# A fused scan and channel-mixer kernel: block 1 of x loaded ahead of w1, b1 from another queue, C loaded behind the first DMA transposes

## Chip, cores, metric

The kernel runs on one core of one Trainium2 chip. The metric is device time in microseconds of one execution. The kernel before was run three times: 159.55, 159.99 and 160.57 us, median 159.99. A further execution was profiled; the times in the views come from that one.

## What is computed

The input x has 2048 rows of 448. It is normalised along the row to xn. One branch (A) is a complex diagonal recurrence over the rows, the other (B) a channel mixer with a second normalisation; their product is added to x:

```python
def _A_ref(x, Lambda_re, Lambda_im, B_re, B_im, C_re, C_im, log_dt, Dskip):
    ...
    Lam_bar = jnp.exp(dt * Lam)
    B_bar = ((Lam_bar - 1.0) / Lam)[:, None] * Bmat
    Bu = jnp.einsum("bld,pd->blp", x + 0j, B_bar)
    ...
    for t in range(L):
        h = Lam_bar[None, :] * h + Bu[:, t, :]
        hs.append(h)
    ...
    y = 2.0 * jnp.einsum("blp,dp->bld", hseq, Cmat).real + x * Dskip[None, None, :]
    return y

def _B_ref(x, w1, b1, w2, b2):
    y = _layernorm(x, axis=-1)
    h = _gelu(jnp.einsum("bsd,df->bsf", y, w1) + b1)
    return jnp.einsum("bsf,fd->bsd", h, w2) + b2

x = A_x
xn = _layernorm(x, axis=-1)
s = _A_ref(xn, ...)
g = _silu(_B_ref(xn, B_w1, B_b1, B_w2, B_b2))
return x + s * g
```

Inputs and output are bfloat16.

## The kernel before

**Tiling.** The rows are cut into 8 blocks of 256 rows; a block lies on 128 partitions as 128 even and 128 odd rows (`par` 0 and 1). Two blocks form a group, and there are 4 groups. The program's loop over groups emits, for each, the statistics and the two normalised forms of x (`xn` for branch A, `xn2`, called `xm` in the keys, for branch B), their transposes (`xnT`, `xn2T`), the products with B (`bu`, L616), the recurrence as scans (`ssm`, L641), the first mixer product with GELU (`mm1`, L686 and L692), the second mixer product (`mm2`, L715), and the output of the recurrence with the final sum (`ym`, L747 to L759).

**Group 0 is different.** Its first mixer product is cut in halves by block (`mm1_half`, L701 and L707): all seven pairs of columns for block 0, then all seven for block 1, so that it can begin when block 0 alone is there. Block 0 is normalised by `first_norm`, each half as soon as it has landed, and transposed on TensorE (L380). Block 1 is normalised by `ln_stats`, `ln_scale` and `ln_apply` on VectorE and transposed by eight matmuls on TensorE (`xt`, L440), whose result VectorE copies out of bank 6 (L446).

**Weights and loads.** w1 is loaded in four chunks of its columns (`ldw1`), each as two DMAs, one of 384 rows (keys `w1_0` to `w1_3`) and one of the remaining 64 (`w1r_0` to `w1r_3`). The bias b1 is one more row of the same tile, on partition 64 (key `w1b`), and every first-mixer product reads it, so every L701 task needs it. The tile's lower half is zeroed first (L293). B comes in four DMAs (`Bn`), w2 in four, C in three (`ldc`, into a part of `gT` that is free at that time; keys `Cn0`, `Cn512`, `Cn448`). Nearly all loads go out from SyncE, in one hardware queue. The four parameter vectors (`vrows`) go out from ScalarE's queue, ahead of its first table load.

**DMA transposes.** VectorE and ScalarE make the scaled B matrices (`lb`, L566 to L569); each is then transposed by a DMA on SyncE (`bt`, keys `BT0` to `BT6`, L83). The transposes of xn for group 0 (`xnT0_0`, `xnT0_1`) and all later transposes of xn and xm are DMA transposes on SyncE as well, and so are those of C (`ct_dma`, keys `Ct0` to `Ct3`). L83 and L84 are the two issuing lines of the helper `dma`; all DMAs carry one of them.

**Order.** All work is a list of tasks, numbered in the order in which the program makes them. A hand-written list, `ORDER`, gives the order in which they are emitted; each engine runs its own tasks in that order. `SECOND` names the tasks that take their second engine. `link` finds what each task depends on from the keys that it reads and writes, and `emit` puts a wait on a semaphore ahead of a task where its engine has not yet seen that the other is done. A wait stops everything behind it on that engine; for SyncE this is every later DMA.

SyncE's order in the start-up, by keys: `x0p0`, `x0p1` (the two halves of block 0), `w1_0`, `w1r_0`, `w1b` (b1), `x1`, `w1_1`, `w1r_1`, `w1_2`, `w1r_2`, `w1_3`, `w1r_3`, four of `Bn`, four of w2, `x2` with `x3` (one DMA), `Cn0`, `Cn512`, `BT3`, `Cn448`, `xnT0_1`, `BT0`, `xnT0_0`, then the two transposes of xm for group 1, then `Ct3`, `Ct0`, `Ct2`, `Ct1`.

TensorE's order: warm-up, parameters, block 0's transposes, six halves of `mm1_half` for block 0, block 1's transposes (task 113), the seventh half for block 0, seven for block 1, four `mm2` of group 0, `bu` with `BT3` and `BT0`, `mm1` of group 1. The chunks are used by two halves each (the last by one).

The lines for the scaled identity `De` (L530 on ScalarE, L531 on VectorE), used by `m0` (L605, L607) with CQ, are part of the start-up too: `De0` and `De1` on VectorE, `De3` and `De2` on ScalarE between GELUs.

Of the kernel before, what the change touches and what calls it, by code (L numbers as in the profile page):

```python
# [17 lines left out]
class Task:  # L18

    __slots__ = ("eng", "ins", "reads", "writes", "sem", "idx", "deps", "chain", "alts")

    def __init__(self, eng, ins, reads, writes, sem):
        self.eng, self.ins, self.reads, self.writes, self.sem = eng, ins, tuple(reads), tuple(writes), sem
        self.deps = set()
        self.chain = False
        self.alts = [(eng, ins)]

    def choose(self, k):  # L30
# [5 lines left out]
class Plan:  # L36
# [4 lines left out]
    def __init__(self, nc):  # L41
        self.nc = nc
        self.engs = {"pe": nc.tensor, "act": nc.scalar, "dve": nc.vector, "pool": nc.gpsimd, "sp": nc.sync}
        self.tasks = []
        self.sems, self.counts, self.cms = {}, {}, []
        for e in ("pe", "act", "dve", "pool"):
            self._sem(e)
        self.seen = {e: {} for e in ENGS}
        self.ndma = 0

    def _sem(self, name):
# [9 lines left out]
    def add(self, eng, ins, reads=(), writes=(), dur=0.2, lat=0.1, prio=0.0, sem=None, chain=False, table=None, mode=None):  # L61
        if callable(ins):
            ins = [ins]
        t = Task(eng, ins, reads, writes, sem or eng)
        t.idx = len(self.tasks)
        t.chain = chain
        self.tasks.append(t)
        return t

# [35 lines left out]

    def emit(self):
        self.link()
        for k in SECOND:
            self.tasks[k].choose(1)
        order = [self.tasks[k] for k in ORDER]  # L110
        assert len(order) == len(set(order)) == len(self.tasks)
        done = {}
        for t in order:
            eng, seen = self.engs[t.eng], self.seen[t.eng]
            need = {}
            for d in t.deps:
                sem, val = done[d]
                if need.get(sem, 0) < val:
                    need[sem] = val
            for sem, val in need.items():  # L120
                if seen.get(sem, 0) < val:
                    eng.wait_ge(self.sems[sem], val)
                    seen[sem] = val
            for k, fn in enumerate(t.ins):
                last = fn(eng)
                if t.chain and k < len(t.ins) - 1:
                    self.counts[t.eng] += 1
                    last.then_inc(self.sems[t.eng], 1)
                    eng.wait_ge(self.sems[t.eng], self.counts[t.eng])
                    seen[t.eng] = self.counts[t.eng]  # L130
            inc = 16 if t.sem not in ENGS else 1
            self.counts[t.sem] += inc
            last.then_inc(self.sems[t.sem], inc)
            done[t] = (t.sem, self.counts[t.sem])
        for sem, val in self.counts.items():
            if val and self.seen["sp"].get(sem, 0) < val:
                self.nc.sync.wait_ge(self.sems[sem], val)


def dram_ap(t, offset, ap):  # L140
    return bass.AP(tensor=t.tensor, offset=offset, ap=ap)
# [1 line left out]

ORDER = [int(k) for k in """
# [17 lines left out]
""".split()]  # L164
SECOND = [int(k) for k in """
44 143 144 148 150 168 172 174 178 180 198 200 204 220 230 232 289 290 317 328 402 404 429 434 435 438 511 512 513 538 539 541 542 544 545 607 611 630
# [12 lines left out]
def bass_recurrent_scan__ssm_conv_s5__mixer_channel_mlp__prompt_kernel(  # L179
# [12 lines left out]
    L, D, F = 2048, 448, 1792  # L192
# [5 lines left out]
    with ExitStack() as es:  # L198
        def SB(name, shape, dtype=BF):
            return es.enter_context(nc.sbuf_tensor(name, shape, dtype))  # L200
# [12 lines left out]
        w1_sb = SB("w1_sb", [128, 4, F])  # L213
# [60 lines left out]
        with nc.Block():  # L274
# [28 lines left out]
            def ld(eng, o, i, writes, nbytes, prio, reads=(), dur=0.45):  # L303
                kb.dma(eng, o, i, reads=reads, writes=writes, prio=prio, nbytes=nbytes, dur=dur)
# [4 lines left out]
            def ldx(b0, n, prio, reads=(), eng="sp"):  # L309
                ld(eng, x_all[:, b0:b0 + n, :, :], dram_ap(A_x, b0 * 256 * D, [[2 * D, 128], [256 * D, n], [D, 2], [1, D]]),  # L310
                   [f"x{b}" for b in range(b0, b0 + n)], n * 256 * D * 2, prio, reads, dur=0.25 + 0.2 * n)
# [10 lines left out]
            S1 = 10 * PINNED  # L322
# [1 line left out]
                ld("sp", x_all[:, 0, par, :], dram_ap(A_x, par * D, [[2 * D, 128], [1, D]]), [f"x0p{par}"], 114688, S1)  # L324
            ldw1(0, S1 + 1)
            ldx(1, 1, S1 + 2)
            ld("sp", w1_sb[64:65, 3, :], dram_ap(B_b1, 0, [[F, 1], [1, F]]), ["w1b"], 4000, S1 + 1)
            for c in (1, 2, 3):
                ldw1(c, S1 + 3)
            for ri, bm in enumerate((A_B_re, A_B_im)):  # L330
# [539 lines left out]
```

## Time and profile before

| | |
|---|---|
| runs: median (lowest to highest) | 159.99 us (159.55 to 160.57) |
| profiled execution, first to last instruction | 159.2 us |
| mean granted TensorE clock | 0.996 |
| TensorE busy | 151.3 us (95%) |
| VectorE busy | 136.9 us (86%) |
| ScalarE busy | 93.2 us (59%) |
| GpSimd busy | 51.5 us (32%) |
| DMA | 14.70 MB, mean 92 GB/s over the span |

Engines in the views: PE is TensorE, DVE VectorE, ACT ScalarE, POOL GpSimd, SP SyncE; a q behind the name is the engine's sequencer, which issues DMAs. In a timeline a row has the start, the length, the engine, the line, the operation, the tiles, the count, and in square brackets the idle time of the engine just before and what ended it. In a list of waits a row has the total, the number of times and the longest. A DMA row ends with the time from issue to landing. The names of tiles are those of the memory: the tiles w1 and w2 both appear as `w_sb`, and the loads of C as `gT`.

### The profile page before, as it was taken

What the parts mean: (1) busy time and instruction counts of PE and PEld (TensorE: products, weight loads), DVE (VectorE), ACT (ScalarE), POOL (GpSimd) and SP (SyncE); (2) the same over time, 40 slices, a digit from 0 to 9 for tenths busy, and PEclk for the clock granted to TensorE, in tenths of its full rate; (3) what the DMA queues carried; (4) which work ended last, traced back from release to release, by engine and by line L of the source; (5) the groups of instructions that cost most, each with busy time, mean ns of one, the idle gap of its engine ahead of it and who ended that gap; (6) DMA issues with size and microseconds to landing.
All of it is one profiled execution on the core that took longest, in us unless ns stands there. A gap on an engine that the chain in (4) does not pass through costs nothing.

```text
span 159.2 us, 2725 instructions
## 1 busy us (share of the span) xinstructions
PE 151.3 (95%) x946; PEld 93.7 (59%) x946; DVE 136.9 (86%) x265; ACT 93.2 (59%) x151; POOL 51.5 (32%) x127
## 2 busy tenths in 40 slices
PE   6959999999999999999999999999989999999990
PEld 6849965565565556566655555576556655555560
DVE  5478969999998799999789999893999599999982
ACT  3839899997779962689835472212456972450200
POOL 5578840007616000038600573302015420060021
PEclk9999999999999999999999999999999999999998
DMA  4999999888980057000210430213401000010032
GB/s 103 260 303 364 315 149 198 139 161 159 276 172 4 0 100 147 0 0 4 48 20 0 120 65 1 57 21 94 116 4 58 0 4 0 0 58 0 0 115 60
DMA packets 31174, 14.70 MB, mean 92 GB/s; under 512 B 24693, under 2 KB 30713, under 8 KB 31162
## 3 DMA queue, kind: packets, MB, share of 16 engines
q1 hardware_dynamic: 30914, 14.26, 39.4%
q0 software_dynamic: 96, 0.23, 0.4%
q8 instruction: 7, 0.11, 0.3%
q10 hardware_dynamic: 152, 0.05, 0.1%
q14 instruction: 5, 0.04, 0.1%
HBM read 6.89 MB, written 1.84 MB: 55 GB/s over the span
## 4 chain that ended last, share of the span: by engine, by line
PE 88%; DMA 7%; SPq 2%; DVE 1%; issue 0%
PE psum L715 27%; PE psum L686 21%; PE psum L616 13%; PE psum L747 12%; PE psum L701 7%; PE psum L750 4%; DMA w_sb<-in_B_w_dram 4%; PE psum L605 3%; DMA xnT<-xn_sb 3%; SPq L84 2%; PE psum L753 1%; PE psum L440 0%; DVE t L756 0%; DVE tmp L759 0%; PE psum L607 0%
## 5 line engine op out<-in xcount | busy, mean ns | idle before, releaser
L715 PE MATMUL psum<-w_sb,gT 128*128 128x448 bf16 x224 | 43.8, 352 | 0.0
L686 PE MATMUL psum<-xn2T,w_sb 128*128 128x512 bf16 x168 | 38.2, 379 | 0.1
L715 PEld LDWEIGHTS psum<-w_sb,gT 128*128 128x128 bf16 x224 | 21.9, 98 | 20.0
L692 ACT ACTIVATE gT<-psum 128x1024 bf16<-128x1024 f32 x21 | 21.4, 1021 | 11.7 <-PE psum L686 11.6
L686 PEld LDWEIGHTS psum<-xn2T,w_sb 128*128 128x128 bf16 x168 | 18.5, 112 | 15.8 <-issue 0.7
L616 PE MATMUL psum<-xnT,BT 128*128 128x256 bf16 x196 | 24.0, 273 | 0.5 <-DMA xnT<-xn_sb 0.5
L616 PEld LDWEIGHTS psum<-xnT,BT 128*128 128x128 bf16 x196 | 19.0, 98 | 5.8 <-DMA xnT<-xn_sb 1.0
L719 ACT ACTIVATE th<-o 128x448 f32<-128x448 f32 x16 | 9.1, 573 | 16.4 <-DVE o L718 16.3
L641 DVE TENSOR_TENSOR_SCAN s_f<-cw,cur,v_sb 128x256 f32<-128x256 f32 x21 | 15.6, 784 | 0.2
L701 PE MATMUL psum<-xn2T,w_sb 128*128 128x256 bf16 x112 | 12.9, 273 | 2.0 <-DMA w_sb<-in_B_w_dram 1.8
L701 PEld LDWEIGHTS psum<-xn2T,w_sb 128*128 128x128 bf16 x112 | 11.8, 112 | 2.8 <-DMA w_sb<-in_B_w_dram 2.0
L620 ACT ACTIVATE u_sb<-psum 128x512 bf16<-128x512 f32 x12 | 7.2, 596 | 10.2 <-PE psum L616 10.0
L731 POOL TENSOR_TENSOR xd<-xn_sb,dbc 128x448 bf16<-128x448 bf16 x4 | 4.8, 1198 | 24.9 <-DVE dbc L339 13.9
L747 PE MATMUL psum<-CZ,h_sb 128*128 128x448 bf16 x56 | 11.9, 352 | 0.0
L756 DVE TENSOR_TENSOR t<-psum,g_sb 128x448 bf16<-128x448 f32 (+2 forms) x17 | 9.9, 589 | 1.7 <-PE psum L750 1.1
L358 DVE BATCH_NORM_STATS2 lnst<-x_all 128x6 f32<-128x448 bf16 x14 | 8.2, 611 | 3.5 <-DMA x_all<-in_A_x_dram 3.5
L720 DVE SCALAR_TENSOR_TENSOR g_sb<-th,o 128x448 bf16<-128x448 f32 x16 | 10.4, 664 | 0.7 <-ACT th L719 0.6
L718 DVE TENSOR_TENSOR o<-psum,b2bc 128x448 f32<-128x448 f32 x16 | 9.7, 614 | 1.3 <-PE psum L715 1.3
L747 PE MATMUL psum<-CQ,h_sb 128*128 128x448 bf16 (+2 forms) x54 | 10.5, 332 | 0.0
L731 POOL TENSOR_TENSOR xr<-xd,g_sb 128x448 f32<-128x448 bf16 x5 | 5.5, 1106 | 14.6 <-DVE tmp L759 14.5
L707 ACT ACTIVATE gT<-psum 128x512 bf16<-128x512 f32 x14 | 8.3, 590 | 3.2 <-PE psum L701 2.9
L731 POOL TENSOR_TENSOR xr<-x_all,xr 128x448 f32<-128x448 bf16 x6 | 6.9, 1156 | 9.2 <-DVE xr L732 9.1
(157 smaller groups left out, 224.8 us busy)
## 6 DMA issues: line engine op xcount, KB each, us to landing
out_dram<-tmp SPq DMA_DIRECT2D x7, 224.0 KB, 2.0
w_sb<-in_B_w_dram SPq DMA_DIRECT2D x3, 448.0 KB, 7.0
x_all<-in_A_x_dram SPq DMA_DIRECT2D x3, 448.0 KB, 4.4
w_sb<-in_B_w_dram SPq DMA_DIRECT2D x3, 384.0 KB, 6.2
gT<-in_A_C_re_dram SPq DMA_DIRECT2D x1, 392.0 KB, 11.6
Bn<-in_A_B_re_dram SPq DMA_DIRECT2D x1, 336.0 KB, 6.5
Bn<-in_A_B_im_dram SPq DMA_DIRECT2D x1, 336.0 KB, 6.4
gT<-in_A_C_im_dram SPq DMA_DIRECT2D x1, 336.0 KB, 12.0
```

Source lines behind the costliest of these rows:

```text
L616: fns = [lambda e, r=r, m=m, d=d: e.matmul(psum[:, 4, r * NK:(r + 1) * NK], BT[:, m, d, :], xnT[:, gx, d, :], start=(d == 0), stop=(d == 6 ...
L641: dve(lambda e, i=i, ri=ri, init=init: e.tensor_tensor_scan(s_f[:, i, ri, :], col(R2, i).to_broadcast([128, NK]), v_sb[:, i, ri, :], init, ...
L686: fns = [lambda e, k=k, d=d: e.matmul(psum[:, b0 + k, :], w1_sb[:, d, fcol(2 * j + k)], rhs[:, d, :, :], start=(d == 0), stop=(d == 3)) fo ...
L692: act(lambda e: e.activation(gT[:, gb, 2 * j:2 * j + 2, :], psum[:, b0:b0 + 2, :], ACT.Gelu_apprx_tanh), [f"ps{b0}", f"ps{b0 + 1}"] + (WK ...
L701: fns = [lambda e, k=k, d=d: e.matmul(psum[:, banks[k], :].rearrange("p (r c) -> p r c", r=2)[:, :, cs], w1_sb[:, d, fcol(2 * j + k)], rhs ...
L715: fns = [lambda e, fi=fi: e.matmul(psum[:, bk, 0:D], gT[:, gb, fi, q * 128:(q + 1) * 128], w2_sb[:, fi, :], start=(fi == 0), stop=(fi == N ...
L718: dve(lambda e: e.tensor_tensor(o2[:, fb, :], psum[:, bk, 0:D], b2bc[:], ALU.add), [f"ps{bk}", "b2bc"], [f"oo{fb}"], 0.62, prio - 76)
L719: act(lambda e: e.activation(th[:, fb, :], o2[:, fb, :], ACT.Tanh, scale=0.5), [f"oo{fb}"] + (WK + WKP if g == 0 else []), [f"th{fb}"], 0. ...
L720: dve(lambda e: e.scalar_tensor_tensor(out=g_sb[:, gs, :], in0=th[:, fb, :], scalar=1.0, in1=o2[:, fb, :], op0=ALU.add, op1=ALU.mult), [f" ...
L731: kb.either(("pool", lambda e, o=o, i0=i0, i1=i1, op=op: e.tensor_tensor(o, i0, i1, op), 1.37, 0.15), ("dve", lambda e, o=o, i0=i0, i1=i1, ...
L747: fns = [lambda e, k=k: e.matmul(psum[:, bk, c0:c1], h_sb[:, hb, k, k0:k0 + 128], cm[:, k, c0:c1], start=(k == 0), stop=False) for k in ra ...
L756: dve(lambda e: e.tensor_tensor(t3[:, fb, c0:c1], psum[:, bk, c0:c1], g_sb[:, gs, c0:c1], ALU.mult), [f"ps{bk}", f"g{gs}"], [f"t3{fb}_{c0} ...
```

## The change

Five things move; the arithmetic and the bytes are the same.

1. On SyncE `x1` (task 26) goes out directly behind block 0, ahead of `w1_0`.
2. b1 (task 27) is issued from ScalarE, as its fifth DMA, in place of SyncE.
3. On TensorE block 1's transposes (task 113) stand ahead of the sixth half of block 0 (task 125) in place of behind it.
4. On ScalarE `De3` and `De2` (tasks 146 and 145) move from among block 0's GELUs to behind the last sine of the tables (task 167).
5. On SyncE `BT3` (task 186) and `xnT0_1` (task 152) stand ahead of all three loads of C (tasks 182, 183, 184). The order is now `x2` with `x3`, `BT3`, `xnT0_1`, `Cn0`, `Cn512`, `Cn448`, `BT0`, `xnT0_0`.

VectorE's and GpSimd's orders are unchanged. The helper gains a `tag` by which a task can be named in `ORDER`; no task has one, so the numbering stays as it was. The diff, with the two orders cut to the places that differ:

```diff
-ORDER = [int(k) for k in """
-0 9 18 22 10 1 19 23 11 16 15 12 89 2 20 24 3 8 17 21 14 25 13 5 27 26 7 90
...
-101 34 51 102 55 53 103 56 35 63 106 115 52 36 57 107 117 108 64 116 37 109 65 110 38 66 58 119 118 105 39 59 121 120 67 40 123 146 111 122 112 41 125
-145 149 124 147 61 45 143 113 62 148 144 60 182 127
...
-74 160 135 75 170 134 76 84 171 137 78 136 79 159 186 81 174 139 169 80 82 138 175 141 86 87 140 85 312 273 88 162 184 310 152 311 142 309 185 314 315
-313 277 316 274 163 317 164 151 165 281 318 166 319 172 278 320 167 321
...
+ORDER = [int(k) if k.isdigit() else k for k in """
+0 9 18 22 10 1 19 23 26 11 16 15 12 89 2 20 24 3 8 17 21 27 14 25 13 5 7 90
...
+111 122 112 41 113 125 149 124 147 61 45 143 62 148 144 60 127
...
+133 83 158 77 132 74 160 135 75 170 134 76 84 171 137 78 136 79 159 186 81 174 139 169 80 82 138 175 141 86 87 140 85 312 273 88 162 310 152
+182 183 184 185 151 311 142 309 314 315 313 277 316 274 163 317 164 165 281 318 166 319 172 278 320 167 146 145 321
...
-            ld("sp", w1_sb[64:65, 3, :], dram_ap(B_b1, 0, [[F, 1], [1, F]]), ["w1b"], 4000, S1 + 1)
+            ld("act", w1_sb[64:65, 3, :], dram_ap(B_b1, 0, [[F, 1], [1, F]]), ["w1b"], 4000, S1 + 1)
```

```diff
     def emit(self):
         self.link()
+        plain = [t for t in self.tasks if t.tag is None]
         for k in SECOND:
-            self.tasks[k].choose(1)
-        order = [self.tasks[k] for k in ORDER]
+            plain[k].choose(1)
+        order = [plain[k] if isinstance(k, int) else self.named[k] for k in ORDER]
```

More of the change, by code (lines that the diff above doesn't have):

```diff
@@ L18 @@
 class Task:
-    __slots__ = ("eng", "ins", "reads", "writes", "sem", "idx", "deps", "chain", "alts")
+    __slots__ = ("eng", "ins", "reads", "writes", "sem", "idx", "deps", "chain", "alts", "tag")
     def __init__(self, eng, ins, reads, writes, sem):
@@ L27, in __init__ @@
         self.chain = False
+        self.tag = None
         self.alts = [(eng, ins)]
@@ L48, in __init__ @@
         self.seen = {e: {} for e in ENGS}
+        self.named = {}
+        self.tag = None
         self.ndma = 0
@@ L64, in add @@
         t = Task(eng, ins, reads, writes, sem or eng)
-        t.idx = len(self.tasks)
         t.chain = chain
+        if self.tag is not None:
+            t.tag = self.tag
+            self.named[self.tag] = t
+            self.tag = None
         self.tasks.append(t)
```

32 rows, old and new, of the table ORDER are left out of this document.

## The prediction

> **What bounds the kernel now.** I read the page first, then the waits of TensorE, the chain of waits, the timelines of TensorE, VectorE, SyncE and ScalarE up to 36 us, and the landings of single DMAs (the DMA view, asked for one short window at a time).
>
> ```profile
> span 159.2 us, 2725 instructions
> ...
> PE 88%; DMA 7%; SPq 2%; DVE 1%; issue 0%
> ```
>
> ```profile
> PE psum L701 <- DMA w_sb<-in_B_w_dram: 1.8, 1, 1.8
> ```
>
> The first fence is the page (span; the chain that ended last, by engine), the second the waits of TensorE. The chain is TensorE for 88%. Once its first real matmul has begun, TensorE stands still once for long: 1.8 us at L701, waiting for a piece of w1. An early microsecond won there reaches the end only if nothing between there and the end is late instead. The timeline of TensorE (start, length, engine, line, operation, count, idle before):
>
> ```profile
> 6.52 1.91 PE L701 MATMUL psum<-xn2T,w_sb 128*128 128x256 bf16 x16 [0.28 <-issue]
> 10.19 3.69 PE L701 MATMUL psum<-xn2T,w_sb 128*128 128x256 bf16 x32 [1.76 <-DMA w_sb<-in_B_w_dram]
> 13.72 0.61 PE L440 MATMUL psum<-ident,xn_sb 128*128 128x128 bf16 x8
> ...
> 31.85 1.69 PE L616 MATMUL psum<-xnT,BT 128*128 128x256 bf16 x14
> 33.66 12.26 PE L686 MATMUL psum<-xn2T,w_sb 128*128 128x512 bf16 x56
> ```
>
> The first 16 matmuls use w1's chunk 0 and end at 8.43; the hole of 1.76 lasts until chunk 1 is there. The eight of L440 are block 1's transposes. The chain of waits shows SyncE issuing in front of that hole:
>
> ```profile
> 1.25 0.42 SPq L84
> ...
> 2.19 0.56 SPq L84
> ...
> 2.80 0.47 SPq L84
> ...
> 3.33 0.36 SPq L84
> ...
> 4.20 5.95 DMA w_sb<-in_B_w_dram
> ```
>
> These are the second half of x block 0 (1.25), the end of w1 chunk 0 (2.19), b1 (2.80), x block 1 (3.33), and the end of w1 chunk 1, issued at 4.20 and landed 5.95 later, at 10.15. The DMA view (size, us from issue to landing), one row for each:
>
> ```profile
> x_all<-in_A_x_dram SPq DMA_DIRECT2D x1, 112.0 KB, 2.1
> ...
> w_sb<-in_B_w_dram SPq DMA_DIRECT2D x1, 64.0 KB, 3.5
> ...
> x_all<-in_A_x_dram SPq DMA_DIRECT2D x1, 224.0 KB, 5.2
> ...
> w_sb<-in_B_w_dram SPq DMA_DIRECT2D x1, 224.0 KB, 9.2
> ...
> x_all<-in_A_x_dram SPq DMA_DIRECT2D x1, 448.0 KB, 10.6
> ...
> gT<-in_A_C_im_dram SPq DMA_DIRECT2D x1, 336.0 KB, 12.0
> ...
> BT<-Bn SPq DMA_TRANSPOSE x1, 6.1
> ...
> xnT<-xn_sb SPq DMA_TRANSPOSE x1, 6.1
> ...
> xnT<-xn_sb SPq DMA_TRANSPOSE x1, 4.7
> ...
> xn2T<-xn_sb SPq DMA_TRANSPOSE x1, 3.4
> ```
>
> So x block 0 is there at 1.25 + 2.1 = 3.3, chunk 0 at 2.19 + 3.5 = 5.7, block 1 at 3.33 + 5.2 = 8.5, chunk 1 at 10.15. On this queue the landings come in the order of issue, so their differences are prices: chunk 0 (448 KB) 2.4 us, block 1 (224 KB) 2.8 us, chunk 1 (448 KB) 1.6 us. Block 1, at half the bytes, is the dearest.
>
> **Block 1 ahead of w1, b1 on ScalarE's queue.** The bytes up to chunk 1 are the same; what can change is the cost of starting. Chunk 1 runs in a full queue: 1.6 us for 448 KB, so 0.8 us for 224 KB. Beyond such rates chunk 0 paid 2.4 - 1.6 = 0.8 us and block 1 paid 2.8 - 0.8 = 2.0 us. Bounds for the landing of chunk 1: only b1's issue slot goes (2.80 to 3.33, 0.53 us): 9.62; the whole excess of block 1 goes: 8.15. I take the row nearest to the new order, that of chunk 0, the load that follows block 0 now: a stream that starts behind another costs 0.8 us. Then block 1 lands at 3.3 + 0.8 + 0.8 = 4.9, chunk 0 at 4.9 + 0.8 + 1.6 = 7.3, chunk 1 at 7.3 + 1.6 = 8.9, which is 1.25 earlier than 10.15; later loads in this queue come 1.25 earlier too.
>
> TensorE pays for that at the front: its first L701 now waits for chunk 0 until 7.3 in place of 6.52. It runs 1.91 us to about 9.26, finds chunk 1 landed, and goes on: 10.19 - 9.26 = **0.93 us won**. Bounds of this term: 1.76 (the hole closes, chunk 0 still in time) and -0.3 (rival below).
>
> Of the issues that move, ScalarE gets b1 behind its four parameter loads, ahead of its table load:
>
> ```profile
> 2.21 1.28 ACT L283 ACT_TABLE_LOAD   x1 [2.21 <-issue]
> 3.80 0.29 ACT L374 ACTIVATE lnw<-lnmv,eps 128x1 f32<-128x1 f32 x1 [0.31 <-DVE lnmv L373]
> ...
> 11.93 0.40 ACT L530 ACTIVATE De<-ident,dcol 128x128 bf16<-128x128 bf16 x1
> ...
> 28.59 1.28 ACT L719 ACT_TABLE_LOAD   x1 [0.27 <-DVE o L718]
> ```
>
> The issue costs 0.47 by SyncE's row; the 0.31 of idle time before 3.80 covers most, and 0.16 reaches the first of two normalisation steps, of which the second sets the end. I count 0; without cover 0.16. The Trainium skill ("DMA: Bandwidth & Descriptors", section "Issuing engines are not separate DMA queues") says that issuing from another engine saves only the sequencer's time. By that alone, with no gain from the order, the sum would be 0.53 instead of 0.93; the 2.0 us of excess at block 1 is more than an issue slot, so the trace does not settle for it.
>
> **Block 1's transposes one task earlier.** They are the same eight matmuls of 0.61 us, now before the second half of chunk 2, so they save TensorE nothing. They need VectorE's normalised block 1:
>
> ```profile
> 8.66 1.15 DVE L358 BATCH_NORM_STATS2 lnst<-x_all 128x6 f32<-128x448 bf16 x2 [2.24 <-DMA x_all<-in_A_x_dram]
> ...
> 12.21 1.44 DVE L424 TENSOR_SCALAR xn_sb<-x_all,lnw 128x448 bf16<-128x448 bf16 x4
> ...
> 22.22 2.21 DVE L358 BATCH_NORM_STATS2 lnst<-x_all 128x6 f32<-128x448 bf16 x4 [1.28 <-DMA x_all<-in_A_x_dram]
> ```
>
> VectorE stood 2.24 us for block 1, the first two of the four at 12.21 are done near 12.9. With block 1 at 4.9 this whole stretch moves by 2.24, to 10.7. TensorE gets there at 9.26 plus three tasks of eight matmuls (3.69/4 each), 12.0: 1.3 us of cover. If block 1 landed after 8 us the cover would be gone, and TensorE would pay the rest.
>
> ScalarE's two scalings of De (0.40 each) go from among the first GELUs to behind the sine tables. The consumer (L607) stands in TensorE's order behind the L686 stretch, so after 33.66 + 12.26 = 45.9. Ahead of 28.59 ScalarE had 0.27 us idle and arrives there about 0.9 + 0.8 earlier, so 0.8 more is covered: 0.
>
> **C behind the first DMA transposes.** SyncE's timeline:
>
> ```profile
> 11.60 0.44 SPq L84 DMA_DIRECT2D x_all<-in_A_x_dram  x1
> ...
> 12.59 1.04 SPq L84 DMA_DIRECT2D gT<-in_A_C_im_dram  x1
> ...
> 19.45 1.33 SPq L83 DMA_TRANSPOSE BT<-Bn  x1
> ...
> 21.45 3.12 SPq L83 DMA_TRANSPOSE xnT<-xn_sb  x1
> ...
> 25.96 1.30 SPq L83 DMA_TRANSPOSE xnT<-xn_sb  x1
> ...
> 30.15 1.31 SPq L83 DMA_TRANSPOSE xn2T<-xn_sb  x1
> ```
>
> C was issued from 12.08 on, and SyncE then stood until VectorE had made the first B matrix (19.45). Now that wait comes ahead of C; queued behind it are xnT block 1, C, the second B, xnT block 0, and the x-normalised transposes of group 1. VectorE reaches that B 2.24 earlier, at about 17.2. Landings before: x blocks 2 and 3 at 11.60 + 10.6 = 22.2, C's second part at 24.6, first B at 25.55, xnT block 1 at 27.55, xnT block 0 at 25.96 + 4.7 = 30.7 (needed at 31.85, slack 1.15), the last transpose of group 1 at 30.15 + 3.4 = 33.55 (needed at 33.66, slack 0.1). The first B came 1 us after C's end though issued 6.1 before, so transposes wait behind copies here.
>
> In the new order the same bytes stand before xnT block 0, and one more change from copies to transposes, priced at that 1 us: 30.7 - 1.25 + 1.0 = 30.45, against 31.85 - 0.93 = 30.92. Covered by 0.5. The Trainium skill ("Advanced Engine Details and Errata", section "X-Bar Transpose (TRN2)") holds transposes as fast as ordinary DMAs; by it the extra change is free, the landing 29.45, and the sum the same 0.93.
>
> What is late next is group 1's transpose, slack 0.1: it hangs on VectorE's statistics at 22.22, which waited 1.28 us for x blocks 2 and 3, and these come 1.25 earlier. So it allows 1.25 + 0.1, more than 0.93. w2's last chunk (the 224 KB row; issued just ahead of 11.60, so landed at about 20.3) is also 1.25 earlier, while its user, TensorE behind L701, is 0.93 earlier. GpSimd's order is untouched.
>
> Sum: -0.93 us, of a span of 159.2. The median of the runs, 159.99, lies 0.8 above that span, taken as constant: 159.99 - 0.93 = **159.1 us**. Its own range, by the first term's bounds 1.76 and 0.5: 158.2 to 159.5.
>
> **The rivals.** *Whole hole closed:* block 1 takes over chunk 0's starting cost and chunk 0 starts in a full queue; chunk 0 lands by 6.5, chunk 1 before 8.43. For it: block 1's excess is large enough. Against: every load behind another has shown some start cost so far. 159.99 - 1.76 = 158.2.
>
> *Only b1's slot:* the excess stays, 0.53 us won: 159.5. This is what the skill's rule on issuing engines gives.
>
> *Nothing won at the front:* block 1 keeps its 2.8 us in its new place. Chunk 0 lands at 3.3 + 2.8 + 2.4 = 8.5, TensorE runs 8.55 to 10.46 and has lost 0.27: 160.3. For it: landings were in order of issue.
>
> *C in front of xnT block 0, the slower side.* How fast C moves there decides:
>
> ```profile
> 8.50:18.00 9.50, 7.81 (x75) 7.54 (x76) 8.46 (x30) 6.93 (x14) 7.74 (x29) 1.00 1.09 340
> 18.00:20.50 2.50, 2.50 (x26) 2.48 (x24) 2.46 (x6) 2.22 (x4) 2.24 (x7) 1.00 1.11 248
> 20.50:24.50 4.00, 4.00 (x27) 2.37 (x25) 2.72 (x8) 3.93 (x6) 1.32 (x3) 1.00 1.20 125
> ```
>
> (Windows; the last number is GB/s.) If C starts only when xnT block 1 has landed: x 2 and 3 at 20.95, first B +1, xnT block 1 +2 (27.55 after 25.55), so 23.95; then C's 784 KB (0.80 MB); then B +1 and xnT block 0 +2.4. At 248 GB/s C takes 3.2 us and the end is 30.55, in time for 30.92. At 125, the rate at which C's tail went, it takes 6.4: 33.75, and TensorE stands 2.8 us: 159.99 - 0.93 + 2.8 = 161.9. It turns at about 220 GB/s. Against it: SyncE can issue C while the transposes still run.
>
> **How the numbers follow.** Forecast 0.48, hole closed 0.16, b1's slot 0.14, nothing won 0.11, C late 0.11. One per cent, about what a measurement of this kernel can tell, is 1.6 us: faster means below 158.4, slower above 161.6. Hole closed gives faster in most of its cases, and a little of the forecast: 0.18. Slower is more than half of C late with a little for what I do not see: 0.08. Within 1%: 0.74. The range is 158.2 to 160.9: the bottom is the closed hole, the top takes in the lost front and C late by half.
>
> **What would show it.** Right: TensorE's hole at L701 split into a later start (near 7.3) and no hole before chunk 1; L358 of block 1 at about 6.5; L358 of blocks 2 and 3 near 21; L686 beginning near 32.7. Wrong: the first L701 after 8; idle time before L616 at 31 or L686 at 33 with a transpose as releaser; landings of C's parts after 28. If L686 begins at 33.66 as before, the front's gain was given back at group 1's transposes.

## The result and the profile after

| | before | changed |
|---|---|---|
| median of 20 runs (lowest to highest) | 159.95 us (159.23 to 160.87) | 159.47 us (158.65 to 160.02) |
| profiled execution: span, time | 159.2 us, not timed itself | 157.7 us, 159.45 us |

The ratio is 0.9962, with a 95% interval of 0.9945 to 0.998: faster by 0.4%, within the 1% that was called no change. In microseconds the medians differ by 0.48; the ratio stands for 0.6, its interval for 0.3 to 0.9. Ratios here leave out the runs that lie more than 1.5% above the fastest of the same kernel; where a kernel varies by more than that, the median of all its runs stands beside it.

Wherever a timed run has its span too, the two lie 1.7 to 1.9 us apart (159.45 against 157.7 here). By that the profiled execution of before was one of about 159.2 + 1.8 = 161.0 us, longer than any of the 20 in the table. So not the whole 1.5 us between the two spans belongs to the change. The page of the changed kernel (span; the chain that ended last, by engine):

```profile
span 157.7 us, 2725 instructions
...
PE 86%; DMA 6%; DVE 3%; SPq 2%; issue 1%
```

VectorE has come onto the chain with 3% where it had 1%. TensorE's timeline shows the start-up:

```profile
6.71 1.91 PE L709 MATMUL psum<-xn2T,w_sb 128*128 128x256 bf16 x16 [0.51 <-DMA w_sb<-in_B_w_dram]
9.09 2.79 PE L709 MATMUL psum<-xn2T,w_sb 128*128 128x256 bf16 x24 [0.47 <-DMA w_sb<-in_B_w_dram]
11.71 0.61 PE L448 MATMUL psum<-ident,xn_sb 128*128 128x128 bf16 x8
12.16 8.02 PE L709 MATMUL psum<-xn2T,w_sb 128*128 128x256 bf16 x72
20.02 10.76 PE L723 MATMUL psum<-w_sb,gT 128*128 128x448 bf16 x56
30.61 1.69 PE L624 MATMUL psum<-xnT,BT 128*128 128x256 bf16 x14
32.64 12.28 PE L694 MATMUL psum<-xn2T,w_sb 128*128 128x512 bf16 x56 [0.33 <-DMA xn2T<-xn_sb]
```

Lines are 8 higher than before (L701 is L709, L686 is L694, L715 is L723). The hole of 1.76 us has become two of about half a microsecond, one for chunk 0 and one for chunk 1. The second mixer product begins at 20.02 where it began at 21.26, and L694 at 32.64 where it began at 33.66: of the 1.24 us won up to L723, 0.22 is gone again at L694, twelve microseconds later, and a wait for a transpose stands there that was not there before. The rest of the difference between the two spans lies at the far end, in a wait near 117 us that only the trace of before has (its waits of TensorE):

```profile
PE psum L616 <- DMA xnT<-xn_sb: 0.5, 1, 0.5
```

1.02 + 0.5 is the 1.5 us. The landings in the changed kernel (DMA view, one row for each):

```profile
x_all<-in_A_x_dram SPq DMA_DIRECT2D x1, 224.0 KB, 3.0
...
w_sb<-in_B_w_dram SPq DMA_DIRECT2D x1, 64.0 KB, 3.9
...
w_sb<-in_B_w_dram SPq DMA_DIRECT2D x1, 64.0 KB, 5.1
...
x_all<-in_A_x_dram SPq DMA_DIRECT2D x1, 448.0 KB, 7.8
...
xnT<-xn_sb SPq DMA_TRANSPOSE x1, 5.3
...
xn2T<-xn_sb SPq DMA_TRANSPOSE x1, 4.8
```

Block 1, issued at 1.72, landed at 4.7; chunk 0's end, issued at 2.67, at 6.6; chunk 1's, issued at 3.90, at 9.0; x blocks 2 and 3, issued at 11.18, at 19.0. xnT block 0 was there at 28.9, well ahead of L624 at 30.61. The last of group 1's transposes, issued at 27.76, came at 32.6. What it stands on is in the chain of waits:

```profile
3.90 5.06 DMA w_sb<-in_B_w_dram
...
20.18 2.66 PE psum L723 x14
...
22.87 0.62 DVE o L726
...
27.12 0.40 DVE xn_sb L432
27.52 0.24 DVE Bn L577
27.76 4.83 DMA xn2T<-xn_sb
```

TensorE's first L723 group ends at 22.84, VectorE adds its bias (L726), then makes the normalisation of group 1, and that is transposed for L694. VectorE's timeline has the wait in this chain:

```profile
6.49 1.16 DVE L366 BATCH_NORM_STATS2 lnst<-x_all 128x6 f32<-128x448 bf16 x2
...
19.39 2.20 DVE L366 BATCH_NORM_STATS2 lnst<-x_all 128x6 f32<-128x448 bf16 x4
...
22.87 0.62 DVE L726 TENSOR_TENSOR o<-psum,b2bc 128x448 f32<-128x448 f32 x1 [1.00 <-PE psum L723]
```

### The profile page after: what moved, and what is told of

Same layout as the page of the kernel before. It is cut to its first block, busy times and chain, and to the rows that moved or that the text cites. A ratio compares the mean times of both kernels' runs of the same rounds, so it can differ in the third digit from the quotient of the medians.

```text
span 157.7 us, 2725 instructions
## 1 busy us (share of the span) xinstructions
PE 151.2 (96%) x946; PEld 93.9 (59%) x946; DVE 137.1 (87%) x265; ACT 93.1 (59%) x151; POOL 51.4 (33%) x127
## 4 chain that ended last, share of the span: by engine, by line
PE 86%; DMA 6%; DVE 3%; SPq 2%; issue 1%
PE psum L694 23%; PE psum L723 22%; PE psum L624 13%; PE psum L755 12%; PE psum L709 7%; PE psum L758 4%; PE psum L613 3%; DMA w_sb<-in_B_w_dram 3%; DMA xn2T<-xn_sb 3%; SPq L90 2%; PE psum L761 1%; DVE xn_sb L432 1%; DVE o L726 1%; PE psum L448 0%; DVE t L764 0%
## 5 line engine op out<-in xcount | busy, mean ns | idle before, releaser
L723 PE MATMUL psum<-w_sb,gT 128*128 128x448 bf16 x224 | 43.8, 353 | 0.0
L694 PE MATMUL psum<-xn2T,w_sb 128*128 128x512 bf16 x168 | 38.4, 380 | 0.4 <-DMA xn2T<-xn_sb 0.3
L723 PEld LDWEIGHTS psum<-w_sb,gT 128*128 128x128 bf16 x224 | 21.9, 98 | 20.0
L694 PEld LDWEIGHTS psum<-xn2T,w_sb 128*128 128x128 bf16 x168 | 18.5, 112 | 16.3 <-DMA xn2T<-xn_sb 0.6
L624 PE MATMUL psum<-xnT,BT 128*128 128x256 bf16 x196 | 24.0, 273 | 0.0
L624 PEld LDWEIGHTS psum<-xnT,BT 128*128 128x128 bf16 x196 | 19.0, 98 | 5.1 <-issue 0.4
L709 PE MATMUL psum<-xn2T,w_sb 128*128 128x256 bf16 x112 | 12.7, 273 | 1.0 <-DMA w_sb<-in_B_w_dram 1.0
L709 PEld LDWEIGHTS psum<-xn2T,w_sb 128*128 128x128 bf16 x112 | 11.8, 112 | 1.5 <-DMA w_sb<-in_B_w_dram 0.7
L726 DVE TENSOR_TENSOR o<-psum,b2bc 128x448 f32<-128x448 f32 x16 | 9.8, 617 | 2.2 <-PE psum L723 2.1
L715 ACT ACTIVATE gT<-psum 128x512 bf16<-128x512 f32 x14 | 8.3, 594 | 2.6 <-PE psum L709 2.3
L432 DVE TENSOR_SCALAR xn_sb<-x_all,lnw 128x448 bf16<-128x448 bf16 x19 | 8.5, 459 | 0.4
```

The source lines that it names most:

```text
L432: on = [("dve", lambda e: e.tensor_scalar(dst, src, rs, nb, op0=ALU.mult, op1=ALU.add), 0.4, 0.12), ("act", lambda e: e.activation(dst, sr ...
L624: fns = [lambda e, r=r, m=m, d=d: e.matmul(psum[:, 4, r * NK:(r + 1) * NK], BT[:, m, d, :], xnT[:, gx, d, :], start=(d == 0), stop=(d == 6 ...
L694: fns = [lambda e, k=k, d=d: e.matmul(psum[:, b0 + k, :], w1_sb[:, d, fcol(2 * j + k)], rhs[:, d, :, :], start=(d == 0), stop=(d == 3)) fo ...
L709: fns = [lambda e, k=k, d=d: e.matmul(psum[:, banks[k], :].rearrange("p (r c) -> p r c", r=2)[:, :, cs], w1_sb[:, d, fcol(2 * j + k)], rhs ...
L723: fns = [lambda e, fi=fi: e.matmul(psum[:, bk, 0:D], gT[:, gb, fi, q * 128:(q + 1) * 128], w2_sb[:, fi, :], start=(fi == 0), stop=(fi == N ...
L726: dve(lambda e: e.tensor_tensor(o2[:, fb, :], psum[:, bk, 0:D], b2bc[:], ALU.add), [f"ps{bk}", "b2bc"], [f"oo{fb}"], 0.62, prio - 76)
```

## The experiments

Twelve experiments; three of them (e5, e9, e10) run a kernel again for a further trace. The table gives, from each trace, when TensorE began its first L701 (the first mixer product of group 0), L715 (the second) and L686 (the first mixer product of group 1), in the line numbers of before; then its wait just ahead of that L686, and the span; beside them the times. Each ratio is taken against runs of before made beside that kernel: their median was 159.95 us for the changed kernel, 160.07 for e1 to e4, 160.29 for e5 to e8, and 159.95 for e12.

| kernel | first L701 | L715 | L686 | wait | span | median (lowest to highest) | ratio, 95% |
|---|---|---|---|---|---|---|---|
| before | 6.52 | 21.26 | 33.66 | 0 | 159.2 | 159.95 (159.23 to 160.87) | 1 |
| e9 before again | 7.37 | 20.85 | 32.98 | 0 | 158.3 | 160.05, one | |
| changed | 6.71 | 20.02 | 32.64 | 0.33 | 157.7 | 159.47 (158.65 to 160.02) | 0.9962, 0.9945 to 0.998 |
| e5 changed again | 7.11 | 19.81 | 32.80 | 0.70 | 157.9 | 159.64 (158.87 to 160.4) | 0.9939, 0.9911 to 0.9968 |
| e1 b1 alone | 8.06 | 21.85 | 33.98 | 0 | 159.3 | 159.91 (159.1 to 161.01) | 0.9987, 0.9954 to 1.0019 |
| e2 block 1 alone | 6.55 | 19.39 | 33.13 | 0.89 | 158.2 | 159.28 (159.02 to 160.02) | 0.9952, 0.9929 to 0.9974 |
| e3 block 1 and b1 | 6.76 | 19.60 | 31.97 | 0 | 157.0 | 159.52 (158.75 to 160.83) | 0.9966, 0.9934 to 0.9998 |
| e4 C alone | 7.08 | 19.93 | 33.05 | 0.83 | 158.1 | 162.22 (159.85 to 164.02) | 1.0054, 1.0008 to 1.01 |
| e10 C alone again | 7.13 | 20.47 | 33.73 | 0.97 | 158.8 | 160.57, one | |
| e11 C, block 1 later | 7.15 | 20.76 | 35.60 | 1.77 | 160.7 | 162.49, one | |
| e6 changed, C in front | 6.90 | 19.59 | 32.97 | 1.09 | 158.1 | 159.64 (158.49 to 160.45) | 0.9952, 0.992 to 0.9984 |
| e7 changed, b1 on SyncE | 7.11 | 19.81 | 32.98 | 0.88 | 158.1 | 159.65 (159.0 to 162.02) | 0.9952, 0.9922 to 0.9981 |
| e8 group 1 first | 6.73 | 19.43 | 32.43 | 0 | 157.8 | 160.24 (159.23 to 160.61) | 0.999, 0.9959 to 1.0022 |
| e12 scales first | 7.00 | 19.69 | 32.30 | 0.33 | 157.4 | 159.12 (158.54 to 159.52) | 0.9948, 0.9922 to 0.9973 |

Two things are read from the table before any single run. From L686's start to the end every trace takes 125.0 to 125.6 us (157.7 - 32.64 = 125.1), so what is left of any edit is in that start. And the executions of one kernel differ in the start-up by as much as the change is worth: before began L715 at 21.26 once and at 20.85 the other time. One trace proves little here; groups of them do.

### The three parts, each alone

b1 from ScalarE alone (e1), x block 1 directly behind block 0 alone (e2), both (e3), C behind the first transposes alone (e4), all from before:

```diff
 e1
-            ld("sp", w1_sb[64:65, 3, :], dram_ap(B_b1, 0, [[F, 1], [1, F]]), ["w1b"], 4000, S1 + 1)
+            ld("act", w1_sb[64:65, 3, :], dram_ap(B_b1, 0, [[F, 1], [1, F]]), ["w1b"], 4000, S1 + 1)
 e2 (e3: with the lines of e1)
-0 9 18 22 10 1 19 23 11 16 15 12 89 2 20 24 3 8 17 21 14 25 13 5 27 26 7 90
+0 9 18 22 10 1 19 23 26 11 16 15 12 89 2 20 24 3 8 17 21 14 25 13 5 27 7 90
 e4
-... 60 182 127 ... 83 183 158 ... 162 184 310 152 311 ...
+... 60 127 ... 83 158 ... 162 310 152 182 183 184 311 ...
```

> The kernel before with one edit: b1 is issued from ScalarE. x block 1 stays behind w1 chunk 0. Theory (the order of block 1 and chunk 0 is what won): only the issue slot of 0.53 us goes, so chunk 1 lands near 9.6, L701's wait for it shrinks from 1.76 to about 1.2, and the time falls by 0.2 to 0.5 us. Rival (b1's issue slot in front of block 1 and chunk 1 is the whole gain): chunk 1 lands near 9.0 and the time falls by as much as with the whole change, 0.4% (0.6 us).

> The kernel before with one edit: x block 1 is issued directly behind block 0; b1 stays on SyncE behind chunk 0. Theory (order): chunk 0 lands near 6.6 and the first L701 starts near 6.7; b1 is the last that it needs, landing about 2 us after its issue at 3.3, which is in time; chunk 1 is issued as late as before but lands near 9.3, L701 goes on near 9.4, and the time falls by 0.3 to 0.8 us. Rival (slot): chunk 1 lands at 10.1 as before, the first L701 is 0.2 later, no gain (within 0.2 us).

> Both front edits, with block 1's transposes, De and C as in the kernel before. Theory (the front is the whole gain, the rest only rides along): L701 goes on near 9.1, xnT block 0 lands before TensorE asks for it near 30.6, group 1's L686 starts near 32.7, time as with the whole change (0.4% below before, 0.6 us). Rival (C's place matters once TensorE is earlier): TensorE waits 0.3 us or more at L616 near 31 for a transpose, and the gain is half or less of that of the whole change.

> The kernel before with one edit: the three loads of C stand behind the first B transpose and the transpose of xn block 1. Theory (no wait of TensorE hangs on it): same time within 0.2 us, L616 at 31.9 and L686 at 33.7 as before. Rival 1 (C's place wins): at least 0.4 us faster. Rival 2 (C in front of xnT block 0 costs): xnT block 0 lands after 31.9, and TensorE waits before L616; slower by 0.5 us or more.

**e1** cannot be told from before (0.9987, 0.9954 to 1.0019). Its trace shows no hole at L701, and chunk 1 was there at 9.0, as the rival had it. But it is no witness for the gain of a slot: it is the longest of e1's runs (161.01), and TensorE came late to L701, at 8.06, since the parameters that it transposes first landed late (its waits of TensorE):

```profile
PE psum L456 <- DMA vrows<-in_A_Dskip_dram: 0.9, 1, 0.9
```

e10, with b1 on SyncE, has 0.7 us of the same wait, so this is not b1's doing alone.

**e2** alone has the whole gain, 0.9952 (0.9929 to 0.9974). Its timeline of TensorE:

```profile
6.55 5.40 PE L701 MATMUL psum<-xn2T,w_sb 128*128 128x256 bf16 x48 [0.28 <-DVE xn2T L384]
...
33.13 12.25 PE L686 MATMUL psum<-xn2T,w_sb 128*128 128x512 bf16 x56 [0.89 <-DMA xn2T<-xn_sb]
```

All 48 matmuls of the front run in one piece: chunk 0 was there at 6.2 and chunk 1 at 8.2. Then 0.40 us is lost inside L715, for a bias sum of VectorE (L718), and 0.89 us ahead of L686. VectorE's timeline says why:

```profile
21.48 2.21 DVE L358 BATCH_NORM_STATS2 lnst<-x_all 128x6 f32<-128x448 bf16 x4 [2.45 <-DMA x_all<-in_A_x_dram]
```

x blocks 2 and 3, the input of group 1, landed at 21.45, only 0.75 earlier than before's 22.2, while TensorE was 1.87 earlier (19.39 for 21.26). **e3**, with b1 on ScalarE as well, gains no more than e2 (0.9966 beside 0.9952, intervals overlapping).

**e4** is slower: by 0.5% in the ratio (1.0008 to 1.01), which leaves out six of its twelve runs, and by 1.3% in the median of all twelve. No wait of TensorE was expected to hang on C's place. Its profile is of a run of 159.93, among its shortest, in which block 1 landed early although it stood behind chunk 0 (6.9; at 8.5 in before), and the front had no hole; yet L686 waits 0.83. Its other runs go up to 164.02. They have no trace, so e10 and e11 look for their cause.

### The changed kernel, with one part taken back or one order changed

The changed kernel again (e5); with C's three loads in front of the transposes again (e6); with b1 back on SyncE (e7); and with VectorE's normalisation of group 1 ahead of the first L726 (e8). In e6, e7, e8 and e12 the lines are one lower than in the changed kernel.

```diff
 e6
-... 79 159 186 81 ... 162 310 152 182 183 184 185 ...
+... 79 159 182 183 186 184 81 ... 162 310 152 185 ...
 e7
-            ld("act", w1_sb[64:65, 3, :], dram_ap(B_b1, 0, [[F, 1], [1, F]]), ["w1b"], 4000, S1 + 1)
+            ld("sp", w1_sb[64:65, 3, :], dram_ap(B_b1, 0, [[F, 1], [1, F]]), ["w1b"], 4000, S1 + 1)
-0 9 18 22 10 1 19 23 26 11 16 15 12 89 2 20 24 3 8 17 21 27 14 25 13 5 7 90
+0 9 18 22 10 1 19 23 26 11 16 15 12 89 2 20 24 3 8 17 21 14 25 27 13 5 7 90
 e8
-313 277 316 274 163 317 164 165 281 318 166 319 172
+313 277 316 317 318 319 274 163 164 165 281 166 172
```

> The changed kernel once more, as the yardstick for the three others on the same chip and for a second trace. Theory (block 1's place removes a wait whose length differs from one execution to the next): again 0.3 to 0.6% faster than before, and a smaller spread of its runs than before has; L686 begins between 32 and 33, a transpose of group 1 being the last that it waits for. Rival (the first trace was a lucky one): a wait of 1 us or more at L701, as before.

> The changed kernel with the three loads of C back in front of the first B transpose (the third behind it). Theory (C's place wins nothing by itself): same time as the changed kernel within 0.3 us; x blocks 2 and 3 land 1 to 2.5 us later (20.3 to 21.5), but VectorE waits for TensorE's first L723 group anyway until near 22.9. Rival (with the front earlier, the earlier x blocks 2 and 3 are needed): group 1's last transpose lands 0.5 us or more later, L694 waits that much longer, 0.5 us slower than the changed kernel.

> The changed kernel with b1 back on SyncE, behind w1 chunk 0. Theory (b1's queue is worth nothing once block 1 stands ahead of w1): same time as the changed kernel within 0.3 us; chunk 0 near 6.2 to 6.6, chunk 1 near 8.2 to 9.0. Rival (the 0.5 us slot counts): chunk 1 lands 0.5 us later than in the changed kernel and the time is 0.3 us or more above it.

> The changed kernel with one move on VectorE: group 1's scales (L409 to L419) and the first two of its normalisations (L432) stand ahead of the first bias sum of the second mixer product (L726), which VectorE waited 1.00 us for. Theory (group 1's last transpose is the next bound, and that wait feeds it): the first transpose of xm is issued about 1 us earlier, L694 follows L624 without a wait of its own (0.33 us in the changed kernel), and the time falls by 0.2 to 0.4 us below the changed kernel. Rival (the transposes themselves take as much longer as they are issued earlier, since C and the B transposes are in flight): L694 begins when it did, time as the changed kernel within 0.2 us.

**e5, e6 and e7** have the same median within 0.01 us (159.64, 159.64, 159.65). With block 1 in front, neither C's place nor b1's queue can be seen in the time. e6 differs from e3 only in the places of block 1's transposes and of De, and its ratio (0.9952 beside 0.9966) does not show these either. e5's trace has no hole in the front at all (its timeline of TensorE):

```profile
7.11 4.56 PE L709 MATMUL psum<-xn2T,w_sb 128*128 128x256 bf16 x40
```

In e6 x blocks 2 and 3 landed at 20.9, later than in the changed kernel, and L693 waited longer than in any other kernel with block 1 in front (its timeline of TensorE):

```profile
32.97 12.28 PE L693 MATMUL psum<-xn2T,w_sb 128*128 128x512 bf16 x56 [1.09 <-DMA xn2T<-xn_sb]
```

C's place has two effects, and the medians show no difference between them: issued in front, its copies run ahead of the first transposes (xnT block 1 landed at 26.2 in e6, at 21.9 in the changed kernel); issued behind, they stand in front of xnT block 0 (27.7 in e6, 28.9 in the changed kernel).

**e8** asks what the wait ahead of L694 is worth. Its timeline of TensorE:

```profile
25.61 5.46 PE L722 MATMUL psum<-w_sb,gT 128*128 128x448 bf16 x28 [0.72 <-ACT WT L560]
...
32.43 12.54 PE L693 MATMUL psum<-xn2T,w_sb 128*128 128x512 bf16 x56
```

The wait ahead of L693 is gone, and 0.72 us stands in the second mixer product instead: its third group needs the bank that VectorE's bias sum frees, and that sum was put behind the normalisation (the row names ScalarE, but VectorE's L725, begun at 24.84, is what ends there). The start at 32.43 is only 0.2 to 0.4 earlier than in the two traces of the changed kernel, and the runs are longer (160.24), where 0.2 to 0.4 us less had been expected. Its profile is of one of its shorter runs, 159.52, so where the others lose more is not shown.

### A late front, and the scales first

Before again (e9) and C alone again (e10), for the spread of the front; C alone with block 1 issued later still, behind chunk 1's end (e11), meant to make the front late; and the changed kernel with only the scales of group 1 (task 317) ahead of the first L726 (e12).

```diff
 e11 (with the lines of e4)
-... 14 25 13 5 27 26 7 90 6 28 4 91 29 97 ...
+... 14 25 13 5 27 7 90 6 28 4 91 29 26 97 ...
 e12
-313 277 316 274 163 317 164 165
+313 277 316 317 274 163 164 165
```

> The kernel before, for a second trace of it. Theory (the 1.76 us hole in the first trace is the long end of something that differs from one execution to the next): block 1 lands anywhere from 6.8 to 8.6, the hole at L701 is between 0 and 1.8 us, and L686 begins between 32.5 and 34.3; from that start to the end the kernel takes 125.1 us, plus a wait of up to 0.6 us near 112 if a transpose there is held up. Rival (the hole is always there): block 1 at 8.5 and 1.7 us again.

> The kernel before with C's loads behind the first B transpose and xn block 1's, once more, for a trace of one of its longer executions (its runs went from 159.9 to 164.0). Theory (C in front of xnT block 0 costs when the front is late): the longer the run, the later xnT block 0 and group 1's transposes land (past 32 and past 34), and TensorE waits for them before L616 or L686. Rival (something far behind the start-up): L686 begins near 33 and the time is lost after 36.

> The kernel before with C's loads behind the two transposes, and block 1 issued behind w1 chunk 1, so that it is late in every execution. Theory (as in the run before this one): block 1 lands near 10, VectorE's chain to the first B ends near 20.5, C lands near 29, xnT block 0 near 32 and group 1's transposes past 34.5; TensorE waits 1 us or more for transposes before L686, which begins past 34.5; about 162 us. Rival: transposes land as before, TensorE only waits for block 1's own transposes (under 1 us), 160 to 161 us.

> The changed kernel with only group 1's scales (L409 to L419) ahead of the first bias sum (L726) on VectorE. Theory (group 1's transposes bound L694; their chain has 1 us of VectorE's waiting in it): the bias sum ends near 24.7, early enough for the third group of L723, the transposes of xm are issued 0.5 to 0.8 us earlier, L694 begins between 31.9 and 32.5, and the time is 0.2 to 0.5 us below the changed kernel. Rival (a 16 KB instruction packet of about 1 us that one DMA engine carries between 27 and 31 us holds the transposes up whenever they are issued): landing and L694 as in the changed kernel, time within 0.2 us of it.

**e9** shows that the hole of the first trace was a large one (timeline of TensorE):

```profile
7.37 1.91 PE L701 MATMUL psum<-xn2T,w_sb 128*128 128x256 bf16 x16 [0.28 <-issue]
9.63 3.79 PE L701 MATMUL psum<-xn2T,w_sb 128*128 128x256 bf16 x32 [0.35 <-DMA w_sb<-in_B_w_dram]
```

Here the hole is 0.35, in part because TensorE came to it 0.85 later. With block 1 behind chunk 0 it was 1.76, 0.35, 0.31 (e10) and none (e4).

**e10 and e11** show two executions with C behind the first transposes. In e10 xnT block 0 landed at 30.1 and the last transpose of group 1 at 33.6. In e11 block 1 came at 8.6 (10 had been expected; before's first trace has 8.5), the first transpose was issued at 18.95, and C's second part (336 KB), issued at 22.3, landed at 30.4. TensorE in e11:

```profile
32.14 1.70 PE L616 MATMUL psum<-xnT,BT 128*128 128x256 bf16 x14 [0.62 <-DMA xnT<-xn_sb]
35.60 12.25 PE L686 MATMUL psum<-xn2T,w_sb 128*128 128x512 bf16 x56 [1.77 <-DMA xn2T<-xn_sb]
```

Both waits are for transposes behind C: 2.39 us together, and 162.49 us for the run; another 0.48 us ahead of L440 is for block 1 itself. How late the front was does not explain the two waits: the first transpose was issued only 0.35 us later than in e10 (18.60), and 0.5 earlier than in before (19.45). What differs is xnT block 1, issued just ahead of C: it took 6.6 us to land where e10's took 3.0. From 22.5 to 25.0 us the DMA moved 70 GB/s in e11 and 199 in e10, while a load that GpSimd issues (dbc) was under way in both. Why it was slow in e11 alone is not shown. SyncE's timeline in e11 shows a second price:

```profile
18.95 1.33 SPq L83 DMA_TRANSPOSE BT<-Bn  x1
...
23.43 4.12 SPq L83 DMA_TRANSPOSE BT<-Bn  x1
```

Issuing the first transpose took 1.33 us, issuing the one behind C 4.12, and all transposes behind it were issued that much later.

**e12** has the lowest median of all, 159.12, but 0.9948 (0.9922 to 0.9973) cannot be told from the changed kernel's ratios, and the two were not run side by side. VectorE no longer waited at L725 and was done with the normalisation at 26.6 (27.5 in the changed kernel), and SyncE took its place (its timeline):

```profile
23.59 2.62 SPq L89 DMA_TRANSPOSE xnT<-xn_sb  x1
26.25 3.40 SPq L89 DMA_TRANSPOSE xn2T<-xn_sb  x2
```

The transposes of group 1 can't go out before xnT block 0 has been issued, which took until 26.2; L693 still waited 0.33.

## Why the prediction was right, and where not

The median, 159.47, is 0.4 above the forecast of 159.1 and inside its range, and the cause that it named, block 1's place, is the one that the runs show: e2, which moves nothing else, has the whole gain. How block 1's place helps was forecast wrongly, and the right size of that term was luck. Of the 0.93 us, 0.48 reached the medians (0.6 by the ratio). Point by point:

- **The front, 0.93 us.** Right in size, by luck. L715 began at 21.26, 20.85, 19.93 and 20.47 with block 1 behind chunk 0 (before, e9, e4, e10: mean 20.63), and at 20.02, 19.81, 19.39, 19.60, 19.59, 19.81, 19.43 and 19.69 with block 1 ahead (changed, e5, e2, e3, e6, e7, e8, e12: mean 19.67). The difference is 0.96, from four traces that spread over 1.3 us and eight over 0.6; e1, with its late parameters, and e11, with block 1 later still, are left out. The two terms inside it were both too large. The start cost of 0.8 us, by which L709 was to begin at 7.3, did not come: chunk 0 was there at 6.2 to 6.9, and L709 began at 6.55 to 7.11; TensorE did wait 0.5 us for chunk 0 in the changed kernel and in e3, but with 6.71 and 6.76 it began between the 6.52 and 7.37 of before and e9. And the hole of 1.76 that was to go was one large case of several; the other three were 0.35, 0.31 and 0. In the changed kernel's own trace 0.47 of it was left; in the seven other traces with block 1 ahead, nothing. Too much paid and too much won came to the same sum.
- **The rivals of the front.** *Nothing won* is out by those means. *Hole closed* is out as a time (158.2), but as a course of events it comes nearer than the forecast: it had chunk 0 there by 6.5 and chunk 1 before 8.43, the forecast had 7.3 and 8.9, and in those seven traces chunk 0 landed at 6.2 to 6.9 and chunk 1 at 8.0 to 8.5. Closing the hole was worth less than 1.76 because it was seldom that large. *Only b1's slot* is not what happened: e2 without any slot saved gains 0.9952, and e7 against e5, which differ in b1's queue alone, are at one median. That equality agrees with the rule in the Trainium skill ("DMA: Bandwidth & Descriptors", section "Issuing engines are not separate DMA queues"): another issuing engine saves sequencer time alone. The order of the loads is what counted. ScalarE's issue took 0.27 us (0.47 estimated), and its first activation came 0.08 later, at 3.88.
- **Block 1's transposes and De, nothing.** Right: L366 of block 1 ran at 6.49 (6.5 foreseen), TensorE took L448 without a wait, and the De scalings end at 27.7, ahead of the table load.
- **C behind the transposes, covered.** Right for this front: xnT block 0 came at 28.9 (30.45 foreseen), against 30.6. Taken alone, C's move has a median of 162.22 over all its runs, beside 161.9 for the rival *C in front of xnT block 0*, and e11 shows that rival's waits (0.62 for xnT block 0, 1.77 for group 1). In the other two traces of C alone xnT block 0 was in time as well (29.6 against 30.52 in e4, 30.1 against 31.06 in e10). So it is not shown that the early block 1 is what covers C's move, nor that e4's long runs went like e11, as none of them was traced.
- **What is late next: the step that failed.** "So it allows 1.25 + 0.1, more than 0.93" was wrong. x blocks 2 and 3 came 3.2 us earlier than in before (19.0 for 22.2), far more than 1.25, yet the last transpose of group 1 came only 0.96 earlier (32.6 for 33.55). Two things lie between. VectorE, which works in order, stood 1.00 us at L726 for TensorE's own first L723 group. And the transpose, issued 2.4 us earlier (27.76 for 30.15), took 4.83 where before had 3.4. SyncE, busy issuing xnT block 0 until 26.3, held the first of these transposes up by only 0.1 here, since its input was ready at 26.25; in e12 SyncE was the one waited for. In e2 and e6 the load itself was the late one (21.45 and 20.9, and VectorE waited 2.45 and 1.87 us for it). So L694 waited 0.33 in the changed kernel, 0.70 in e5, 1.09 in e6, 0.88 in e7, 0.89 in e2, and not at all in e3: its start has a mean of 32.75 in these six, against 33.32 for before and e9. That is 0.57 us, or 0.4% of 160, as the runs show. In the same eight traces L715 begins 1.35 us earlier (19.70 against 21.06) and the last transpose of group 1 lands 0.5 us earlier (32.67 against 33.18): more than half of what the front won there was gone by L694. With two traces of before that share is rough; the 0.96 of the larger group would make it two fifths.
- **The sum against the profile.** "The median lies 0.8 above that span, taken as constant" was wrong: the offset is 1.8, and the span was that of a long execution. It did no harm, since 0.93 was taken from the median; a sum made against 159.2 + 1.8 would have been 1 us too long. It does explain why the hole in the first trace looked so dear. "One per cent, about what a measurement of this kernel can tell" was too coarse: twenty runs a side told 0.4%.
- **Transposes as fast as copies.** The rule weighed here (the Trainium skill, "Advanced Engine Details and Errata", section "X-Bar Transpose (TRN2)") is not settled by the start-up. In the changed kernel xnT block 0, 224 KB, took 5.3 us from issue to landing, but behind C, and its landing at 28.9 lies nearer to the 29.45 that this rule gave than to 30.45. At the quiet end of the kernel a transpose of a block took 2.9 us (DMA view of the changed kernel near 111 us):

```profile
xnT<-xn_sb SPq DMA_TRANSPOSE x1, 2.9
```

Stores of the same 224 KB took 2.0 (the page of the changed kernel):

```profile
out_dram<-tmp SPq DMA_DIRECT2D x7, 224.0 KB, 2.0
```

By these two rows a transpose is the slower one, against the rule, and the measurement decides. They are not quite like for like, since the stores write `out_dram` and these transposes go from one tile to another; a plain copy from tile to tile is in none of the traces.

## What to carry to other kernels

Put the load whose consumer chain is longest first in a shared queue, and settle it by groups of traces: one trace may show a start-up hole five times as large as the next. Follow an early microsecond through every engine that works in order, to the next operation that stands behind it: here about half of the gain ended in group 1's transposes, whose producer waited now for a load, now for the very engine that had been sped up. A move that cannot be seen in the time together with another can cost alone (here 0.5% in the ratio, 1.3% in the median of all runs), so undo the parts one by one before keeping them.

## What the runs showed of the hardware

**Transposes that stand still beside an instruction fetch.** In every trace a packet of 16 KB of the kind "instruction" (taken here for a fetch of program code) runs for 0.9 to 1.4 us somewhere between 26 and 34 us. In the changed kernel's packet records it begins at 28.69 and lasts 1.07 us. The windows of the changed kernel (start and end, the engines' busy time, clock, DMA share; the last number is GB/s):

```profile
28.00:29.00 1.00, 1.00 (x7) 0.54 (x6) 0.93 (x3) 0.99 (x2) 0.00 (x0) 1.00 1.32 298
29.00:30.00 1.00, 1.00 (x7) 0.50 (x6) 0.74 (x2) 1.00 (x3) 0.00 (x0) 1.00 2.10 43
30.00:31.00 1.00, 1.00 (x9) 0.65 (x7) 0.87 (x3) 0.97 (x3) 0.00 (x0) 1.00 0.65 138
31.00:32.00 1.00, 1.00 (x11) 0.90 (x10) 1.00 (x2) 0.96 (x3) 0.00 (x0) 1.00 1.82 276
```

Group 1's transposes were under way; from 29.2 to 30.5 next to nothing of them moved, and then they went on at the old rate. The wait of 0.5 us near 117 us in before has the same company: the transpose issued at 112.32 took 4.65 us, beside 2.9 in the changed kernel, and a fetch of 0.88 us began at 114.91. All fourteen traces have this transpose. In twelve no such fetch ran beside it, and it took 2.9 us in each; in e1 a fetch began half a microsecond after its issue, and it took 3.3. A fetch does not always cost: between 87 and 92 us one began within the last microsecond of a transpose in every trace, and that transpose took 2.9 to 3.0 us (the one issued next took 3.3 to 3.8, beside 3.0 to 3.3 for one near 77 us). A standstill of the same look, without a 16 KB fetch, lies behind C's copies (26.2 to 27.1 in the changed kernel). Both would fit transposes that wait for the slowest of the earlier packets. That cause is argued from the timing alone; the fetches moved by themselves from one execution to the next, and no run moved one.

**Behind large loads the issue itself is dear**: a transpose took 1.2 us to issue at the quiet end (at 112.32 in before), 2.7 us behind C in the changed kernel, and 4.1 behind C in e11.

**The first loads vary from one execution to the next**: the same 224 KB of block 1, in the same place, took 5.2 us from issue to landing in before, 4.8 in e9, and 3.5 in e4.
